# Rotary attention in front of two gated layers: how the first two head pairs are prepared, a second raw area, and a new order of the planned work

## The chip, the cores and the metric

One Trainium2 chip, of which the program uses one core. The metric is device time of one execution, in microseconds (us); of several executions the median is given. Lower is better.

## The reference

Inputs are q, k, v (4 batches, 8 heads, 576 positions, width 64), a dense gated layer and an eight-expert layer. Cut to what matters:

```python
q_rot, k_rot = (rotate(q), rotate(k))          # rotary: x*cos + swapped(x)*sin
scores = np.matmul(q_rot, k_rot.transpose(0, 1, 3, 2)) / sqrt(64)
attn = exp(scores - max) / (sum + 1e-9)
x = np.matmul(attn, v)                         # -> (2304, 512)
gate = 1 / (1 + exp(-(x @ w_gate)))            # 512 -> 1536
x = (gate * (x @ w_val)) @ w_out
e = argmax(x @ wg2 + bias[modality])           # one of 8 experts per token
out = prob[e] * (relu(x @ w1[e]) @ w2[e])
```

Everything is float32 outside. Inside, most factors are split into a high part in TensorE's fast 32-bit type and a remainder ("hi" and "lo"), and a product is the sum of hi·hi, lo·hi and hi·lo.

## The kernel before, in words

The program has three stages: attention for 16 head pairs (4 batches of 4 pairs), the gated layer, and routing with the experts. The change touches attention alone.

A **pair** is two heads side by side on 128 partitions, 64 for each. Its nine score **tiles** have 128 queries against 576 keys each: four for head 0, four for head 1, one for what is left of both. The steps of a pair, with the lines of the code as it was before:

- **Loads** (`plan_loads`, L344): raw q and k with a half-swapped copy of each, by SP's queue, into the area `sa` (`self.raw`), of which there is one. The load of pair p waits until the last reader of pair p−1 (`lo`) is through.
- **Preparation**: rotary products and their sum (L175, L177, L173), high part (L165, L397, L409), low part (L451, L399, L411). Scores want, in one operand, a head's high queries on its 64 partitions and the low ones on the other 64 (`q2`), against the high keys on both (`kh`); the low keys `kl` get a second product. From pair 2 on (`plan_prep`) both heads are split at once on 128 partitions, and six small DMAs (L461) put the parts where the scores want them. Pairs 0 and 1 (`plan_direct`) have no time for these DMAs: ACT and DVE write each part in its place, 64 partitions at a time.
- **Scores** (`scores`, L198): four or six matmuls of 288 columns into PSUM, two tiles in flight. For pair 0 the low keys are met by 64 partitions of queries, `(q[r], kl[r])`. DVE takes the scores out of PSUM with the row maximum (`evac_scores`, L208), ACT does the exponential with the row sum (L220).
- **Transposes** on TensorE (L251, L266), split by ACT (`pth`, L281) and DVE (`ptl`, L285); **values** (L298) in four groups per pair; ACT and DVE put them into `xy` (L306, L316, `value_add`).
- **Norm**: reciprocal of the row sums (L228), transposed and written out and read back along rows by DMA (L233, L504, L240), multiplied in (`normalise`, L245).
- **Fillers**: the conversion of the gated layer's first weights from 64-bit words (L650 to L685), and at the end the first two blocks of the gated layer (`early`, L725).

The **order** is set by a planner (`Plan`). Every step is entered with an engine, a cost, the steps that it needs and a priority; the planner goes through the program in modelled time and takes, on each engine, the ready step with the lowest number. The emitted order is fixed from then on: an engine runs its steps in that order and waits on semaphores for what is not there. The priorities come from a table of offsets (`PR`, `OFF`), and which engine does a movable step from other tables (`LO`, `VLO`, `ROPE`, `RM`, `HI`, `VHI`, `DIRECT`, `KLO`). DVE and POOL steps with two operands in SBUF are marked as shared: the planner lets only one of them run at a time.

Of the kernel before, what the change touches and what calls it, by code (L numbers as in the profile page):

```python
# [7 lines left out]
F32 = mybir.dt.float32  # L8
# [19 lines left out]
def f32(ap):  # L28
    return ap.bitcast(F32)
# [92 lines left out]
class Attention:  # L122
    def __init__(self, tc, pool, xpool, psum_s, psum_t, psum_v, qk, v, rope, ident, xt, rows, idle):
# [16 lines left out]
        self.raw = f32(sa[:, 0:4 * S]).rearrange("p (a s) -> p a s", a=4)  # L140
# [6 lines left out]
        self.vraw = t([128, 10, D], F32, "vraw")  # L147
        for i in range(2):
            nc.vector.memset(f32(self.q2[i][:, 0, S:640]), 0.0)
            nc.vector.memset(f32(self.q2[i][:, 1, 0:64]), 0.0)  # L150
            for x in range(2):
                nc.vector.memset(f32(self.w[i][64 - 64 * x:128 - 64 * x, S * x:S * x + S]), 0.0)
# [16 lines left out]
    def rope_op(self, eng, j, what, c=slice(0, S)):  # L169
        e = self.engine(eng)  # L170
        raw = self.raw
# [7 lines left out]
    def scores(self, T):  # L179

        nc = self.nc
# [4 lines left out]
        if t == 8:  # L188
            mm = [(q2[:, x, 512 * (1 - x):512 * (1 - x) + 128], kh[:, x]) for x in range(2)]
            mm.append((self.w[i][:, 512:640], kl))  # L190
        else:
            j, x = divmod(t, 2)
            r = slice(64 * x, 64 * x + 64)
            q = q2[:, x, 128 * (j + x):128 * (j + x) + 128]
            mm = [(q, kh[:, x]), (q[r], kl[r]) if p == 0 else (self.w[i][:, 640 * x + 128 * j:640 * x + 128 * j + 128], kl)]
# [141 lines left out]
    def plan_loads(self, p, load_rope=None, load_const=None):  # L337
        nc = self.nc
        b, hp = divmod(p, NP)
        at = TPP * (p - 2) + 1  # L340

        def ld(half, cols):
            h = slice(2 * half, 2 * half + 2)
            return lambda: nc.sync.dma_start(out=self.raw[:, h, cols], in_=self.qk[b, hp, :, h, cols])  # L344
# [11 lines left out]
    def plan_v(self, p):  # L356
# [5 lines left out]
        self.op(("vhi", p), eng, {"ACT": 0.62, "POOL": 0.76}[eng], lambda eng=eng: self.copy(eng, vv[:, :, 0], self.vraw),  # L362
                [("loadv", p)] + prev, pr)
        eng = self.VLO.get(p, "POOL")
        self.op(("vlo", p), eng, {"DVE": 0.74, "POOL": 1.58}[eng], lambda: self.engine(eng).tensor_tensor(
# [8 lines left out]
    def plan_direct(self, p, pr):  # L374

        nc = self.nc
        q2, kh, kl, w_, raw = self.q2[p], self.kh[p], self.kl[p], self.w[p], self.raw
        cost = lambda eng, w: {"DVE": 0.07 + w / 960, "POOL": 0.12 + w / 465, "ACT": 0.093 + w / 1200}[eng]
        r = [slice(0, 64), slice(64, 128)]
        every = {0: [], 1: []}  # L380
        need = {}
        for half in (1, 0):
            j = 2 * half
            for n, c in enumerate(self.cuts(p, half)):
                w = c.stop - c.start
                load = [("load", p, half, n)] + [("rope", i) for i in range(len(self.cuts(0, 1))) if c.stop > SH * i]
                for k, what in enumerate(("mul", "mul", "add")):
                    e = "POOL" if (p, half, n, k) in self.DIRECT else "DVE"
                    i = j + 1 - k if k < 2 else j
                    self.op(("rope", p, half, n, k), e, cost(e, w), lambda e=e, i=i, what=what, c=c: self.rope_op(e, i, what, c),  # L390
                            load if k < 2 else [("rope", p, half, n, 0), ("rope", p, half, n, 1)], pr + n)
                rot = [("rope", p, half, n, 2)]
                if half:
                    for x in range(2):
                        for y in range(2):
                            self.op(("khi", p, y, x, n), "ACT", cost("ACT", w),
                                    lambda x=x, y=y, c=c: nc.scalar.copy(out=kh[r[y], x, c], in_=raw[r[x], 2, c]), rot, pr + 1 + x + n)  # L397
                        e = "POOL" if (p, x, n) in self.KLO else "DVE"
                        self.op(("klo", p, x, n), e, cost(e, w), lambda e=e, x=x, c=c: self.engine(e).tensor_tensor(  # L399
                            out=kl[r[x], c], in0=raw[r[x], 2, c], in1=f32(kh[r[x], x, c]), op=ALU.subtract),  # L400
                            [("khi", p, x, x, n)], pr + 2 + x + n)
                        keys = [("khi", p, 0, x, n), ("khi", p, 1, x, n), ("klo", p, x, n)]
                        every[1] += keys
                        need.setdefault(("k", x), []).extend(keys)
                    continue
                for x in range(2):
                    i, o = c, slice(c.start + 64 * x, c.stop + 64 * x)
                    key = (p, x, c.start)
                    self.op(("qhi", *key), "ACT", cost("ACT", w), lambda x=x, o=o, i=i: nc.scalar.copy(  # L409
                        out=q2[r[x], x, o], in_=raw[r[x], 0, i]), rot, pr + 1.5 + x + n)  # L410
# [1277 lines left out]
```

## Time and profile before

| | us |
|---|---|
| median of 3 runs | 1044.75 (1043.98 to 1047.44) |
| the profiled execution | 1046.64 |
| its span, first to last instruction | 1044.8 |
| PE (TensorE) busy in the span | 990.2 (95%) |
| DVE (VectorE) busy | 673.5 (64%) |
| ACT (ScalarE) busy | 529.4 (51%) |
| POOL (GpSimd) busy | 360.1 (34%) |
| attention, up to the last value products | about 317 |

The shares are over the whole program. A stage is read from windows: there the busy time of each engine stands for one stretch of the span, with TensorE's granted clock (1.00 is the upper of its two levels, 2.4 GHz; 0.50 the lower, 1.2 GHz).

### The profile page before, as it was taken

What the parts mean: (1) busy time and instruction counts of PE and PEld (TensorE: products, weight loads), DVE (VectorE), ACT (ScalarE), POOL (GpSimd) and SP (SyncE); (2) the same over time, 40 slices, a digit from 0 to 9 for tenths busy, and PEclk for the clock granted to TensorE, in tenths of its full rate; (3) what the DMA queues carried; (4) which work ended last, traced back from release to release, by engine and by line L of the source; (5) the groups of instructions that cost most, each with busy time, mean ns of one, the idle gap of its engine ahead of it and who ended that gap; (6) DMA issues with size and microseconds to landing.
All of it is one profiled execution on the core that took longest, in us unless ns stands there. A gap on an engine that the chain in (4) does not pass through costs nothing.

```text
span 1044.8 us, 16293 instructions
## 1 busy us (share of the span) xinstructions
PE 990.2 (95%) x6035; PEld 912.2 (87%) x6035; DVE 673.5 (64%) x1208; ACT 529.4 (51%) x1042; POOL 360.1 (34%) x276
## 2 busy tenths in 40 slices
PE   4789999989999999999999999999987999999996
PEld 3779999888998999999999999999965899999995
DVE  7799999999997746545535535523376755555651
ACT  5889898988886522212212212223331645555542
POOL 2458768766412423223223323301151012111111
PEclk9899999999999999999999999999998899999998
DMA  5387776856311311101101101000046877666650
GB/s 193 105 224 211 191 197 175 227 165 181 106 65 63 101 41 42 62 21 61 41 21 61 42 20 61 21 1 2 1 137 186 307 228 232 221 222 223 222 170 24
DMA packets 66198, 127.23 MB, mean 122 GB/s; under 512 B 6511, under 2 KB 29695, under 8 KB 66112
## 3 DMA queue, kind: packets, MB, share of 16 engines
q1 hardware_dynamic: 52192, 108.55, 34.3%
q0 software_dynamic: 3040, 9.70, 2.7%
q10 hardware_dynamic: 10880, 7.87, 2.5%
q8 instruction: 49, 0.80, 0.3%
q14 instruction: 37, 0.30, 0.1%
HBM read 95.65 MB, written 9.77 MB: 101 GB/s over the span
## 4 chain that ended last, share of the span: by engine, by line
PE 53%; issue 18%; DVE 11%; DMA 7%; ACT 5%; POOL 3%; SPq 0%; ACTq 0%; POOLq 0%; DVEq 0%
PE gv L725 28%; PE yo L791 13%; DMA out<-e_y,r_si 5%; DVE e L208 3%; PE pv L298 3%; PE s L198 3%; DVE ptl L285 2%; ACT e L220 2%; PE pt L251 2%; ACT pth L281 1%; POOL e_xg L1456 1%; DMA sa<-in_qk 1%; DVE xy L316 1%; PE s L725 1%; PE r_pl L1225 1%
## 5 line engine op out<-in xcount | busy, mean ns | idle before, releaser
L734 POOL TENSOR_TENSOR gl<-sg,gh 128x384 fp32r<-128x384 f32 x60 | 63.5, 1059 | 259.0 <-ACT gh L733 259.0
L732 DVE TENSOR_TENSOR sg<-gv,sg 128x384 f32<-128x384 f32 x70 | 39.1, 558 | 142.0 <-PE gv L725 122.1
L220 ACT ACTIVATE e<-e,st 128x576 f32<-128x576 f32 x144 | 112.0, 781 | 17.9 <-DVE e L208 17.0
L1449 DVE TENSOR_TENSOR e_w<-wr,e_w 128x1024 fp32r<-128x1024 f32 x80 | 96.0, 1222 | 28.3 <-ACT e_w L1448 26.8
L208 DVE TENSOR_SCALAR_CACHE_REDUCE e<-s 128x576 f32<-128x576 f32 x144 | 105.2, 746 | 6.8 <-PE s L198 6.1
L731 ACT ACTIVATE sg<-gv 128x384 f32<-128x384 f32 x70 | 34.4, 491 | 144.8 <-PE gv L725 144.6
L251 PE MATMUL pt<-cst,e 128*128 128x128 f32 x576 | 83.1, 280 | 12.5 <-DVE ptl L285 7.1
L285 DVE TENSOR_TENSOR ptl<-pt,pth 128x512 fp32r<-128x512 f32 x144 | 93.3, 680 | 1.9 <-ACT pth L281 0.6
L1448 ACT CAST e_w<-wr 128x1024 fp32r<-128x1024 f32 x80 | 81.5, 1048 | 23.7 <-DMA x_rows<-xy 20.3
L198 PE MATMUL s<-sb 128*128 128x288 f32 x320 | 77.3, 333 | 16.3 <-DVE sb L411 12.1
L1504 PE MATMUL e_py<-e_w,e_hh 128*128 128x512 f32 x288 | 89.6, 392 | 0.0
L1519 POOL DMA_INDIRECT out<-e_y,r_si x19 | 19.6, 1030 | 188.3 <-ACT e_y L1518 177.9
L281 ACT CAST pth<-pt 128x512 fp32r<-128x512 f32 x144 | 79.1, 586 | 9.7 <-PE pt L251 9.0
L251 PEld LDWEIGHTS pt<-cst,e 128*128 128x128 f32 x576 | 69.1, 144 | 16.7 <-issue 5.5
L1486 PE MATMUL e_ph<-e_xh,e_w 128*128 128x256 f32 x576 | 82.4, 287 | 0.7 <-ACT e_xh L1469 0.7
L733 ACT CAST gh<-sg 128x384 fp32r<-128x384 f32 x60 | 30.8, 514 | 100.8 <-DVE sg L732 100.8
L298 PE MATMUL pv<-pth,vv 128*128 128x256 f32 (+1 forms) x256 | 74.2, 312 | 6.4 <-DVE xy L316 5.4
L725 PE MATMUL gv<-xe,wb 128*128 128x384 f32 x384 | 78.9, 338 | 0.0
L1486 PEld LDWEIGHTS e_ph<-e_xh,e_w 128*128 128x128 f32 x576 | 76.3, 195 | 1.7 <-ACT e_xh L1469 1.1
L725 PE MATMUL gv<-xh,wb 128*128 128x384 f32 x288 | 74.1, 338 | 0.0
L175 POOL TENSOR_TENSOR sa<-sa,rope 128x1152 f32<-128x1152 f32 x24 | 64.1, 2672 | 28.1 <-DMA sa<-in_qk 21.1
L198 PEld LDWEIGHTS s<-sb 128*128 128x128 f32 x320 | 51.2, 200 | 22.8 <-DVE sb L411 12.1
(247 smaller groups left out, 2471.5 us busy)
## 6 DMA issues: line engine op xcount, KB each, us to landing
wr<-in_w SPq DMA_DIRECT2D x74, 512.0 KB
sa<-in_qk SPq DMA_DIRECT2D x30, 576.0 KB
sb<-sa SPq DMA_DIRECT2D x56, 288.0 KB
wraw<-in_wg SPq DMA_DIRECT2D x12, 512.0 KB
wraw<-in_wv SPq DMA_DIRECT2D x12, 512.0 KB
wraw<-in_wo SPq DMA_DIRECT2D x12, 512.0 KB
vraw<-in_v SPq DMA_DIRECT2D x16, 320.0 KB
rr<-recip_rows SPq DMA_DIRECT2D x32, 144.0 KB
```

The lines of the kernel that those rows point to most:

```text
L198: nc.tensor.matmul(ps[:, u, 0:SH], a, m[:, SH * u:SH * u + SH], start=n == 0, stop=n == len(mm) - 1)
L208: self.nc.vector.tensor_scalar(out=e, in0=ps[:, :, 0:SH], scalar1=-0.125, scalar2=3.0e38, op0=ALU.mult, op1=ALU.min, accum_out=st[:, 0])
L220: nc.scalar.activation(out=e, in_=e, func=AF.Exp, bias=st[:, 0], scale=-1.0, accum_out=st[:, 1])
L251: nc.tensor.transpose(pt[:, c], e[:, 128 * c:128 * c + 128], self.ident)
L281: self.nc.scalar.copy(out=hi, in_=src)
L285: self.nc.vector.tensor_tensor(out=lo, in0=src, in1=f32(hi), op=ALU.subtract)
L298: nc.tensor.matmul(ps[:, 0:w], a, m, start=n == 0, stop=n == len(mm) - 1)
L725: self.nc.tensor.matmul(p[:, 0:U], a[:, wc], b[:, c], start=c == 0 and n == 0, stop=c == KC - 1 and n == 2)
L791: nc.tensor.matmul(ps, a, b, start=n == 0, stop=n == 3 * len(GROUPS[grp]) - 1)
L1449: nc.vector.tensor_tensor(out=lo, in0=raw, in1=f32(hi), op=ALU.subtract)
L1486: nc.tensor.matmul(ps[:, k], a[:, fs], b[:, c], start=n == 0, stop=n == 3 * KC - 1)
L1504: nc.tensor.matmul(ps, a[:, f, hs], b, start=n == 0, stop=n == 23)
```

## The change

- **Pair 0's queries** are kept as they lie: the high parts of both heads in one array of 128 partitions, the low parts in another, each written by one operation per piece. So that one head's keys do not meet the other head's queries, `kh` and the low keys (now `kl0`, in the area `w`) have zeros on the other 64 partitions. A tile is then six matmuls over 128 partitions (hi·hi, lo·hi, hi·lo), twelve for the last; high keys are copied once rather than twice. The zeros come from memsets, of which POOL now does some.
- **Unread products** (`warm`): 14 matmuls of 128 x 320 in plain float32 on zeros, ahead of the first score; nobody reads them.
- **Pair 1** goes the way of the later pairs (`plan_prep`), with products, sums and low parts on POOL and six placing DMAs. A tiny POOL addition (`first`) that reads pair 0's last results is put ahead of them, so that POOL starts on pair 1 only when pair 0 is prepared.
- **A second raw area** for odd pairs up to 11, in the part of `xy` that the last batch will fill: a load of pair p waits for pair p−2 there. Even pairs and the last four use `sa`.
- The priorities and the engine tables are **set anew**; the first two blocks of the gated layer get their planned ends behind the last values.

The diff, cut to its core:

```diff
-        self.raw = f32(sa[:, 0:4 * S]).rearrange("p (a s) -> p a s", a=4)
+        self.raws = [f32(sa[:, 0:4 * S]).rearrange("p (a s) -> p a s", a=4), xt[:, :, (B - 1) * S:B * S]]
...
+        nc.vector.memset(self.xv, 0.0)
+        o = [slice(64, 128), slice(0, 64)]
+        for x in range(2):
+            nc.vector.memset(f32(self.kh[0][o[x], x]), 0.0)
+            nc.vector.memset(f32(self.w[0][o[x], S * x:S * x + S]), 0.0)
...
+    def half_of(self, p):
+        return p % 2 if p < (B - 1) * NP else 0
...
+        if p == 0:
+            h, l, z = q2[:, 0], q2[:, 1, 64:640], self.kl[0]
+            if t < 8:
+                c = 128 * j + 64 * x
+                own = [(h[:, c:c + 128], l[:, c:c + 128], x)]
+            else:
+                own = [(h[:, 512:640], z[:, 128:256], 0), (z[:, 0:128], q2[:, 1, 0:128], 1)]
+            mm = [a for qh, ql, x in own for a in ((qh, kh[:, x]), (ql, kh[:, x]), (qh, self.kl0[x]))]
...
-                self.dma(("load", p, half, n), size, ld(half, cols), [("lo", p - 1, half)], at)
+                self.dma(("load", p, half, n), size, ld(half, cols), [("lo", q, half) for q in before], at)
...
-                        for y in range(2):
-                            self.op(("khi", p, y, x, n), "ACT", cost("ACT", w),
-                                    lambda x=x, y=y, c=c: nc.scalar.copy(out=kh[r[y], x, c], in_=raw[r[x], 2, c]), rot, pr + 1 + x + n)
+                        self.op(("khi", p, x, n), "ACT", cost("ACT", w),
+                                lambda x=x, c=c: nc.scalar.copy(out=kh[r[x], x, c], in_=raw[r[x], 2, c]), rot, pr + o_["kh"] + o_["x"] * x + o_["n"] * n)
...
+                self.op(("qhi", p, n), "ACT", cost("ACT", w), lambda hi=hi, c=c: nc.scalar.copy(out=hi, in_=raw[:, 0, c]),
+                        rot, pr + o_["qh"] + o_["n"] * n)
+                self.op(("qlo", p, n), "DVE", cost("DVE", w), lambda hi=hi, lo=lo, c=c: nc.vector.tensor_tensor(
+                    out=lo, in0=raw[:, 0, c], in1=f32(hi), op=ALU.subtract), [("qhi", p, n)], pr + o_["ql"] + o_["n"] * n)
...
+        self.op("first", "POOL", 0.1, self.first, every[0] + every[1], -500)
...
-    VLO = dict.fromkeys((2, 5, 6, 7, 12, 14, 15,), "DVE")
-    ROPE = dict.fromkeys(((2, 0), (3, 1), (4, 0), (11, 1),), "DVE")
+    VLO = dict.fromkeys((0, 4, 10, 12, 13,), "DVE")
+    ROPE = dict.fromkeys(((2, 0), (2, 1), (9, 1),), "DVE")
...
+    def warm(self, n=14):
+        ps = self.ps_t.tile([128, 512], F32, name="warm", tag="pt", bufs=PT_BUFS)
+        for _ in range(n):
+            self.nc.tensor.matmul(ps[:, 0:320], self.xv[:, 0:128], self.xv, start=True, stop=True)
...
-                if p + 1 < self.NDIRECT:
-                    self.plan_direct(1, 0.0)
-                else:
-                    self.plan_prep(p + 1)
+                self.plan_prep(p + 1)
```

Three places of the emitted order follow. In the names, `s` are score tiles in PSUM, `e` the scores out of it, `pt` and `ptl` transposed tiles and their low parts, `sb` holds `q2` and `kh`, `sa` the raw area, `w_99`/`w_100` the arrays `w`, `wr` borrowed weight space (there `kl` of pair 0 and `p5`).

TensorE (PE), the start of the program, as it was before the change:

```order
L198 MATMUL s<-sb 128x288 x2
L198 MATMUL s<-wr,sb 128x288 x2
L198 MATMUL s<-sb 128x288 x2
L198 MATMUL s<-wr,sb 128x288 x2
L198 MATMUL s<-sb 128x288 x2
```

The same engine and place now:

```order
L576 MATMUL warm<-xv 128x320 x14
L222 MATMUL s<-sb 128x288 x4
L222 MATMUL s<-w_99,sb 128x288 x2
L222 MATMUL s<-sb 128x288 x4
L222 MATMUL s<-w_99,sb 128x288 x2
```

Fourteen unread products now stand first, and a tile is four matmuls with `kh` and two with the low keys, where it was two and two.

DVE, between the middle score tiles of pair 0 and its transposed tiles, as it was:

```order
L208 TENSOR_SCALAR e,st<-s 128x576
L177 TENSOR_TENSOR sa<-sa,rope 128x576
L208 TENSOR_SCALAR e,st<-s 128x576 x2
L173 TENSOR_TENSOR sa<-sa 128x576
L177 TENSOR_TENSOR sa<-sa,rope 128x576
L285 TENSOR_TENSOR ptl<-pt,pth 128x4x128
L285 TENSOR_TENSOR wr<-pt_216,wr 128x256
L208 TENSOR_SCALAR e,st<-s 128x576
L399 TENSOR_TENSOR kl_98<-sa,sb 64x576
L208 TENSOR_SCALAR e,st<-s 128x576 x2
L411 TENSOR_TENSOR sb<-sa,sb 64x576 x2
L285 TENSOR_TENSOR ptl<-pt,pth 128x4x128 x3
```

DVE now, from pair 0's first score tile to its ninth:

```order
L390 TENSOR_TENSOR vv_95<-vraw,vv_95 128x10x64
L232 TENSOR_SCALAR e,st<-s 128x576 x5
L309 TENSOR_TENSOR ptl<-pt,pth 128x4x128
L232 TENSOR_SCALAR e,st<-s 128x576
L309 TENSOR_TENSOR ptl<-pt,pth 128x4x128
L309 TENSOR_TENSOR wr<-pt_246,wr 128x256
L232 TENSOR_SCALAR e,st<-s 128x576 x2
L309 TENSOR_TENSOR ptl<-pt,pth 128x4x128 x2
L232 TENSOR_SCALAR e,st<-s 128x576
L190 TENSOR_TENSOR sa<-sa,rope 128x1152
```

The six steps of pair 1 (L177, L173, L399, L411) are gone from between the evacuations; all nine tiles of pair 0 are taken out before a rotary product of pair 2 (L190).

POOL, its work from pair 0's low values on, as it was:

```order
L365 TENSOR_TENSOR vv_95<-vraw,vv_95 128x10x64
L177 TENSOR_TENSOR sa<-sa,rope 128x576 x2
L173 TENSOR_TENSOR sa<-sa 128x576
L399 TENSOR_TENSOR kl_98<-sa,sb 64x576
L365 TENSOR_TENSOR vv_96<-vraw,vv_96 128x10x64
```

POOL now, from its last step for pair 0 on:

```order
L188 TENSOR_TENSOR sa<-sa 128x320
L451 TENSOR_TENSOR order<-w_99,sb 128x2
L190 TENSOR_TENSOR xy<-xy,rope 128x2x576 x2
L188 TENSOR_TENSOR xy<-xy 128x576 x2
L473 TENSOR_TENSOR sa<-xy,sa 128x576
L473 TENSOR_TENSOR kl_98<-xy,sa 128x576
```

All of pair 1's products, sums and low parts now stand on POOL in one run, behind the tiny addition L451; their raw area is `xy`.

## Rows read from the trace of the kernel before

**Rows 1.** Windows: busy us (instructions) of each engine, granted clock, DMA share and rate

```profile
core 0: us, PE busy (x) PEld busy (x) DVE busy (x) ACT busy (x) POOL busy (x), PEclk, DMA share, GB/s
0.00:317.00 317.00, 281.80 (x2040) 264.62 (x2041) 291.36 (x653) 261.01 (x606) 189.17 (x124) 0.98 0.60 170
13.87:40.28 26.41, 20.38 (x73) 16.11 (x74) 20.22 (x37) 16.58 (x35) 10.25 (x7) 0.89 0.45 143
12.06:31.45 19.39, 17.96 (x58) 13.12 (x58) 14.78 (x31) 13.52 (x29) 7.97 (x5) 1.00 0.33 105
36.03:40.96 4.93, 4.90 (x22) 4.93 (x23) 3.39 (x6) 3.50 (x8) 1.84 (x2) 0.50 0.75 233
40.28:300.82 260.54, 243.53 (x1859) 232.31 (x1859) 248.96 (x565) 227.14 (x536) 173.96 (x110) 0.99 0.63 173
320.00:680.00 360.00, 359.51 (x1904) 337.86 (x1903) 194.56 (x290) 109.87 (x207) 104.37 (x91) 1.00 0.15 46
```

**Rows 2.** DVE group, 14 to 40.3 us (busy us, mean ns | idle before, releaser)

```profile
L208 DVE TENSOR_SCALAR_CACHE_REDUCE e<-s 128x576 f32<-128x576 f32 x10 | 7.5, 752 | 4.8 <-PE s L198 4.7
```

**Rows 3.** Timeline of PE: start us, length us, what; three places

```profile
30.10 1.10 PE L198 MATMUL s<-sb 128*128 128x288 f32 x4
39.56 0.68 PE L198 MATMUL s<-kl,w 128*128 128x288 f32 x2
298.41 0.77 PE L198 MATMUL s<-sb 128*128 128x288 f32 x4
```

**Rows 4.** DVE groups by shape, 0 to 310 us

```profile
L177 DVE TENSOR_TENSOR sa<-sa,rope 128x576 f32<-128x576 f32 x2 | 1.5, 752 | 0.0
L173 DVE TENSOR_TENSOR sa<-sa 128x576 f32<-128x576 f32 x5 | 3.8, 750 | 0.0
L399 DVE TENSOR_TENSOR kl<-sa,sb 64x576 fp32r<-64x576 f32 x1 | 0.7, 744 | 0.0
L411 DVE TENSOR_TENSOR sb<-sa,sb 64x576 fp32r<-64x576 f32 x2 | 2.9, 1438 | 0.1
L411 DVE TENSOR_TENSOR sb<-sa,sb 64x320 fp32r<-64x320 f32 x2 | 1.4, 707 | 0.1
L411 DVE TENSOR_TENSOR sb<-sa,sb 64x256 fp32r<-64x256 f32 x2 | 0.8, 419 | 0.1
L173 DVE TENSOR_TENSOR sa<-sa 128x320 f32<-128x320 f32 x1 | 0.5, 492 | 0.0
L175 DVE TENSOR_TENSOR sa<-sa,rope 128x1152 f32<-128x1152 f32 x4 | 6.3, 1566 | 0.1
L365 DVE TENSOR_TENSOR vv<-vraw,vv 128x640 fp32r<-128x640 f32 x7 | 6.2, 885 | 0.1
L451 DVE TENSOR_TENSOR sa<-sa 128x576 fp32r<-128x576 f32 x3 | 5.6, 1879 | 0.8 <-ACT sa L165 0.8
```

**Rows 5.** PE group of plain float32 products on constants, 320 to 1044 us

```profile
L1412 PE MATMUL e_ph<-cst 128*128 128x512 f32 x16 | 7.0, 592 | 0.0
```

**Rows 6.** POOL groups by shape, 0 to 310 us

```profile
L175 POOL TENSOR_TENSOR sa<-sa,rope 128x1152 f32<-128x1152 f32 x24 | 64.1, 2672 | 28.1 <-DMA sa<-in_qk 21.1 <-ACT e L220 5.3 <-DMA sb<-sa 1.7
L173 POOL TENSOR_TENSOR sa<-sa 128x576 f32<-128x576 f32 x25 | 36.9, 1477 | 2.8 <-DVE sa L177 2.0
L451 POOL TENSOR_TENSOR sa<-sa 128x576 fp32r<-128x576 f32 x11 | 16.3, 1483 | 13.7 <-ACT sa L165 13.3
```

**Rows 7.** Chain of waits, 200 to 240 us: a placing DMA in it

```profile
204.70 5.43 DMA sb<-sa
```

**Rows 8.** Timeline around 228 us, and the windows row behind it

```profile
226.17 2.67 POOL L175 TENSOR_TENSOR sa<-sa,rope 128x1152 f32<-128x1152 f32 x1 [5.32 <-ACT e L220]
226.64 2.81 DVE L451 TENSOR_TENSOR sa<-sa 128x576 fp32r<-128x576 f32 x1
...
230.79 1.25 PE L251 MATMUL pt<-cst,e 128*128 128x128 f32 x8 [2.29 <-DVE ptl L285]
...
231.79:235.50 3.71, 3.71 (x21) 3.52 (x20) 2.41 (x5) 1.74 (x4) 1.94 (x2) 0.55 1.02 283
```

More of the change, by code (lines that the diff above doesn't have):

```diff
@@ L167, in copy, with raw, rope_op @@
             self.nc.gpsimd.tensor_scalar(out=out, in0=in_, scalar1=1.0, scalar2=0.0, op0=ALU.mult, op1=ALU.add)
-    def rope_op(self, eng, j, what, c=slice(0, S)):
+    def half_of(self, p):
+        return p % 2 if p < (B - 1) * NP else 0
+    def raw(self, p):
+        return self.raws[self.half_of(p)]
+    def rope_op(self, eng, p, j, what, c=slice(0, S)):
         e = self.engine(eng)
-        raw = self.raw
+        raw = self.raw(p)
         if what == "add":
@@ L339, in plan_loads @@
         b, hp = divmod(p, NP)
-        at = TPP * (p - 2) + 1
+        at = TPP * p - self.PR["load"]
+        before = [q for q in range(p) if self.half_of(q) == self.half_of(p)][-1:]
         def ld(half, cols):
             h = slice(2 * half, 2 * half + 2)
-            return lambda: nc.sync.dma_start(out=self.raw[:, h, cols], in_=self.qk[b, hp, :, h, cols])
+            return lambda: nc.sync.dma_start(out=self.raw(p)[:, h, cols], in_=self.qk[b, hp, :, h, cols])
         for half in (1, 0) if p == 0 else (0, 1):
@@ L361, in plan_v @@
         eng = self.VHI.get(p, "ACT")
[L362 removed]
+        self.op(("vhi", p), eng, {"ACT": 0.62, "POOL": 0.70}[eng], lambda eng=eng: self.copy(eng, vv[:, :, 0], self.vraw),
                 [("loadv", p)] + prev, pr)
         eng = self.VLO.get(p, "POOL")
[L365 removed]
+        self.op(("vlo", p), eng, {"DVE": 0.74, "POOL": 1.53}[eng], lambda: self.engine(eng).tensor_tensor(
             out=vv[:, :, 1], in0=self.vraw, in1=f32(vv[:, :, 0]), op=ALU.subtract), [("vhi", p)], pr)
@@ L421, in plan_direct @@
                             need.setdefault((x, t), []).extend(keys)
-                    every[0] += keys
-                    last = slice(512 - 512 * x, S - 512 * x)
-                    if p == 0 and c.start <= last.start < c.stop:
-                        self.op(("qd", p, x), "ACT", 0.15, lambda x=x, last=last: nc.scalar.copy(
-                            out=w_[r[x], 512 + 64 * x:576 + 64 * x], in_=raw[r[x], 0, last]), rot, pr + 8)
-                        every[0].append(("qd", p, x))
+                every[0] += keys + [("qz", p, n)]
+        self.op("first", "POOL", 0.1, self.first, every[0] + every[1], -500)
         for half in range(2):
@@ L430, in plan_direct, with first @@
         self.ready[p] = [need[t % 2, t // 2] + need["k", t % 2] for t in range(8)] + [every[0] + every[1]]
+    def first(self):
+        self.nc.gpsimd.tensor_tensor(out=self.stat1, in0=f32(self.w[0][:, S - 1::S]), in1=f32(self.q2[0][:, 1, 319::320]), op=ALU.add)
     def plan_prep(self, p):
@@ L483, in plan_tile @@
         ready = self.ready[p][t]
-        self.op(("s", T), "PE", (0.81 if t == 8 else 0.54 if p else 0.92) * (1 if T > 4 else 2), lambda: self.scores(T), ready, T + o["s"], "s")
+        self.op(("s", T), "PE", 0.27 * (2 + (p == 0)) if t < 8 else 0.81 * (1 + (p == 0)), lambda: self.scores(T), ready, T + o["s"], "s")
         self.op(("tsa", T), "DVE", 0.665, lambda: self.evac_scores(T), [("s", T)], T + o["tsa"], "e")
@@ L773, in early @@
             gh, gl = (w[:, 0:U] for w in self.w[1][2 - u])
-            deps = [prev, ("post", u - 1, 3), "table"]
+            deps = [prev, ("post", u - 1, 3), "table"] + [("value", last, x, w) for x in range(2) for w in range(2)]
             for n, (eng, cost, _) in enumerate(self.gv_post(0, u, None, sg, gh, gl, "DVE")):
```

84 lines of the change are left out of this document (41 added, 43 removed).

## The prediction, made before the changed kernel ran

> **What bounds the kernel now.** I read the windows first [rows 1]. Behind 320 us TensorE is busy 359.5 of 360 us: what follows attention is bound by TensorE and does not change, so every microsecond by which attention ends earlier comes out at the end, and every one later too. In attention (0 to 317 us) it is DVE that is nearly full: 291.4 us busy, against 281.8 of TensorE and 261.0 of ACT. From 40 to 301 us DVE is idle for only 260.5 − 249.0 = 11.6 us, TensorE for 17, ACT for 33. So attention lasts as long as DVE's work and the gaps in it, and the question about each part of the change is what it does to these two.
>
> The gaps lie unevenly. From the first evacuation of scores (13.87 us) to the tenth, pair 1's first (40.28 us), DVE is idle 26.4 − 20.2 = 6.2 us [rows 1]; 4.7 us of that it waits for scores from TensorE [rows 2]. TensorE in turn is busy 18.0 of 19.4 us from 12 to 31 us, but slowly: four score matmuls of 288 columns take 1.10 us at 30.1 us and 0.77 us at 298.4 us [rows 3]. At 39.6 us two of them take 0.68 us [rows 3], in a stretch where the granted clock is 0.50, the lower level [rows 1]. The clock column reads 1.00 from 12 to 31 us, but the pace is that of the lower level, and I go by the pace.
>
> The Trainium skill weighs against this reading: "TensorE: Matmul & The Clock Gate" (Part 1, What's actually happening) says that TensorE starts throttled and that sustained matmul work releases it. By that rule, pair 0's own 19 us would have lifted the clock early, the unread products would buy nothing, and the sum below would lose its second term and come to −9.4 us. The trace does not agree: the pace at 30 us is still the slow one.
>
> **The change part by part, in DVE's time.**
>
> *Pair 1 leaves DVE.* Two rotary products of 576 columns (1.5 us), one sum (0.75), one low-key step (0.74) and two low-query steps (2.9) go to POOL: −5.9 us [rows 4].
>
> *Pair 0 in natural layout.* Four low-query pieces (1.4 + 0.8 = 2.2 us) become two with the same columns on twice the partitions. DVE's time follows columns here: a 128 x 320 sum takes 0.49 us, a 64 x 256 piece 0.42 [rows 4]. So the two cost between 0.84 and 1.4, I take 1.1. Two low-key pieces come over from POOL, at some 0.45 each (between the same rows), and a 128 x 320 sum goes to POOL (−0.5). Together −0.7 us.
>
> *The engine tables.* Rotary products on DVE go from four to three (−1.57) and their sums with them (−0.75); low values from seven to five (−1.8) [rows 4]. Low parts go from six to seven. Such a step takes 0.74 us where nothing holds it (the low-key step) and 1.88 us on average for three of them [rows 4]; I take 1.3. Together −2.8 us. The fifth of each, the normalisations on DVE, the evacuations and the splits keep their numbers.
>
> The first term is thus −5.9 − 0.7 − 2.8 = **−9.4 us**.
>
> *The unread products and the six-matmul tile.* TensorE has nothing to do until 12.06 us [rows 1]. Eight plain float32 products of 512 columns took 7.0 us at the upper level [rows 5], so 14 of 320 take 7.0 × 4480/4096 = 7.7 us there, and twice that, 15.3, at the lower. They can start once DVE has zeroed the operand, a little after 1 us. In the one stretch that shows a return, the clock came back after 4.9 us of work (36.03 to 40.96 us) [rows 1]; with that I get about 5 us at the lower level, 5 at the upper, and an end near 11.3 us, ahead of the first score. If so they cost nothing; their cover is TensorE's wait for pair 0's preparation, and if it is shorter than they are, the excess delays every score. A tile of six matmuls takes at the upper level under 0.77 × 6/4 = 1.2 us (the row holds the time in which the last result comes out, which the next tile covers), near DVE's 0.75 for taking one out [rows 2, 3]; at the lower level up to 1.10 × 6/4 = 1.65. Of the 4.7 us that DVE waited for scores, then, between 0 and 4.7 return. I take 4.0, since nothing else in that stretch made it wait for long: second term **−4.0 us**.
>
> *Pair 1 on POOL.* In POOL's queue stand two double products, two sums and two low parts: 2 × 2.67 + 2 × 1.48 + 2 × 1.48 = 11.3 us [rows 6]. They begin behind the tiny addition, when pair 0's low parts are there, near 14 us, and end near 25. Six placing DMAs follow on SP, one issue behind the other, and one such transfer stood 5.4 us in the chain of waits [rows 7]: pair 1's scores can start between 29 and 34 us. DVE has pair 0's nine evacuations, nine splits, two products and two sums of pair 2 ahead of pair 1's first tile in the new order; without gaps that is 19 us of work, to about 34. So the DMAs hide, just. What is late next if they don't is pair 1's first tile, and TensorE idles. I cost it at zero, with 0 to 4 us kept for the range. POOL is off the path otherwise (189 of 317 us busy [rows 1]).
>
> *The second raw area* takes away POOL's waits for loads (21.1 us [rows 6]). No engine that is full waits for POOL there, so I cost it at nothing: it lets preparation run ahead.
>
> *ACT* gets five more high parts of values and loses some ten copies of pairs 0 and 1; with 33 us of slack [rows 1] this is nothing.
>
> *The new order* between 40 and 301 us has no price in any row. Its bounds are DVE's idle time there: it could return all of 11.6 us, or add as much. I take zero, the middle, as both orders come from the same planner.
>
> **The sum:** −9.4 − 4.0 = −13.4 us. The profiled execution took 1046.64 us, so it becomes 1033.2. The median of the runs shown is 1044.75, 1.9 us lower, and against it I predict **1031.3 us**. A check inside: DVE's tenth evacuation near 35 us, not 40.3. A measurement of this kernel can tell some 0.3%, about 3 us, from no change.
>
> **Rivals.**
>
> *POOL holds DVE (slower).* At 226 us a rotary product on POOL took 2.67 us, and a low part that DVE began 0.5 us later took 2.81 us instead of 0.74; TensorE then idled 2.3 us and came back at the lower level, granted clock 0.55 from 231.8 to 235.5 us [rows 4, 8]. One such hold costs DVE 2.1 us. The change gives POOL pair 1 as well, and leaves DVE some twenty two-operand steps to be caught. From 13.4/2.1, between six and seven holds more than now, nothing is left of the gain; eight more give 1031.3 + 16.8 = 1048. For it: every step keeps a place that only a modelled time sets. Against it: DVE has fewer such steps than before. The Trainium skill states the mechanism as a rule ("SBUF — State Buffer", Who interferes with whom): a DVE instruction with two SBUF inputs and a POOL instruction that reads SBUF exclude each other for the whole instruction. The trace agrees, by the 2.81 us.
>
> *The clock does not rise.* The products stay at the lower level, end near 16.6 us, delay the first score by 4.5 us, and pair 0 keeps the slow pace. Then the second term is lost and 4.5 us added: −9.4 + 4.5 = −4.9, 1040. For it: the slow pace held for 19 us of work in the present trace. Against it: these products are dense and of full height, as the work from 36 us on was.
>
> *The slow pace had another cause than the clock*, as by the rule above: the scores of pair 0 came slowly because of their 64-partition products, and with six full ones per tile TensorE is no faster. The second term is lost, the first stands: 1044.75 − 9.4 = 1035.3. Against it: full products at 30.1 us were as slow [rows 3].
>
> *The gain is taken back.* The new order makes DVE wait in 40 to 301 us for what it gained at the start, through ACT or through placing DMAs: idle time there doubles, +11.6, and 1043 comes out, no change.
>
> *The new order is also tighter.* Half to all of the 11.6 us go as well: 1020 to 1026.
>
> **How the numbers follow.** Forecast (1026 to 1038) 0.60; slow pace of another cause (1035.3) 0.06; tighter order 0.12; clock that does not rise 0.09; gain taken back 0.07; POOL holds DVE 0.06. Faster by over 0.3% are the first four: 0.87; same 0.07; slower 0.06. The range of 8 in 10 reaches from 1023 (part of the tighter order) to 1040 (the clock rival's own value); it leaves out the last two cases and the far ends of the others.
>
> **What would show it.** Right: score matmuls of pair 0 at the upper pace from 12 us on; DVE idle under 3 us before the tenth evacuation, and that near 35 us; DVE's busy time up to the last value products near 282 us instead of 291; from 320 us on the same times, shifted by 13. Wrong: low parts and normalisations on DVE of 2 to 3 us each with TensorE idle behind them; a long wait of TensorE for pair 1's placing DMAs; unread products that still run when the first queries are ready; or an attention that ends as before, with the idle time moved.

## The result, and the profile after

The changed kernel takes 1033.46 us (median of 4 executions, 1032.35 to 1034.64) beside 1044.88 before: ratio 0.9887, interval 0.9865 to 0.9909. Predicted were 1031.3 us and 1023 to 1040. The profiled execution took 1034.64 us, against 1033.2 of the sum. Against its own median the change brings 1044.88 − 1033.46 = 11.4 us, where 13.4 was forecast. Single executions of one kernel lie several us apart (before: 1042 to 1054 on one chip), so below medians are compared for the end, and profiles stretch by stretch.

The windows of the changed kernel: from the start to the first product of the next gated layer, from the first to the tenth evacuation, from there to the last, and from there to that first product.

```profile
core 0: us, PE busy (x) PEld busy (x) DVE busy (x) ACT busy (x) POOL busy (x), PEclk, DMA share, GB/s
0.00:307.56 307.56, 289.12 (x2108) 270.24 (x2108) 281.58 (x646) 260.14 (x605) 196.93 (x131) 0.99 0.65 179
14.42:35.67 21.25, 18.02 (x123) 16.58 (x123) 17.86 (x38) 15.82 (x36) 15.00 (x10) 0.92 0.61 177
35.67:281.15 245.48, 234.63 (x1787) 223.31 (x1788) 232.79 (x544) 221.47 (x522) 175.77 (x108) 0.99 0.70 188
281.15:307.56 26.41, 24.69 (x161) 22.38 (x159) 20.19 (x45) 17.97 (x40) 2.57 (x2) 1.00 0.18 53
```

The same first stretch of the kernel before, which reached its first product of the gated layer at 321.01 us, and its last stretch, from the last evacuation to that product:

```profile
0.00:321.01 321.01, 285.32 (x2058) 267.43 (x2058) 293.82 (x659) 263.78 (x610) 189.17 (x124) 0.98 0.59 168
300.82:321.01 20.19, 19.61 (x125) 17.75 (x123) 15.05 (x34) 13.20 (x28) 2.72 (x2) 1.00 0.21 68
```

The next layer begins 321.01 − 307.56 = 13.45 us earlier; the sum said 13.4. In this execution it is made up otherwise than the sum: DVE works 293.82 − 281.58 = 12.2 us less (−9.4 predicted) and idles 27.2 − 26.0 = 1.2 us less (−4.0 predicted). A second profile of the same kernel, below, splits its 14.0 us as 9.1 and 4.9, so one profile does not settle the split. By stretches, 5.2 us went from the first to the tenth evacuation and 15.1 from there to the last (260.5, [rows 1], to 245.5; 16.2 of DVE's work), while the last stretch grew by 6.2 us (20.19 to 26.41), where TensorE now works 24.69 us instead of 19.61, and the first evacuation came 0.55 later. What follows took 725.1 us instead of 723.8. The granted clock falls there in both kernels, at different places (after the change between 772 and 804 us and again from 1024 us on; before it between 768 and 816 us and from 1036 on); that these falls make the difference was not shown.

The DVE groups that answer to [rows 4], and one more of before (the normalisations) behind them:

```profile
L390 DVE TENSOR_TENSOR vv<-vraw,vv 128x640 fp32r<-128x640 f32 x5 | 5.3, 1054 | 0.0
L269 DVE TENSOR_TENSOR xy<-xy,rr 128x576 f32<-128x576 f32 x5 | 5.1, 1023 | 0.0
L473 DVE TENSOR_TENSOR sa<-sa 128x576 fp32r<-128x576 f32 x2 | 4.7, 2336 | 0.0
L190 DVE TENSOR_TENSOR sa<-sa,rope 128x1152 f32<-128x1152 f32 x2 | 2.8, 1418 | 0.0
L190 DVE TENSOR_TENSOR xy<-xy,rope 128x1152 f32<-128x1152 f32 x1 | 1.4, 1361 | 0.0
L433 DVE TENSOR_TENSOR sb<-sa,sb 128x256 fp32r<-128x256 f32 x1 | 1.1, 1082 | 0.0
L192 DVE TENSOR_TENSOR sa<-sa,rope 128x320 f32<-128x320 f32 x2 | 0.9, 482 | 0.0
```

```profile
L245 DVE TENSOR_TENSOR xy<-xy,rr 128x576 f32<-128x576 f32 x5 | 6.3, 1263 | 0.0
```

Five normalisations cost 1.2 us less though nothing about them changed; the rotary products are shorter too, the low values longer (1054 ns each, 885 in [rows 4]). POOL seems to hold some of DVE's steps less often in the new order and others more, and the clock does not fall near 232 us as in [rows 8]. Where it does hold DVE, the prices are as before: two low parts of 2336 ns, and a low query of 1082 ns that would take some 0.42.

TensorE at the start, with its score products at line 222:

```profile
1.26 9.69 PE L576 MATMUL warm<-xv 128*128 128x320 f32 x28 [1.26 <-DVE xv L148]
11.55 0.53 PE L222 MATMUL s<-sb 128*128 128x288 f32 x2 [0.60 <-ACT sb L431]
13.86 0.42 PE L222 MATMUL s<-w,sb 128*128 128x288 f32 x2
15.23 1.26 PE L222 MATMUL s<-sb 128*128 128x288 f32 x4 [0.95 <-DVE e L232]
33.57 0.52 PE L222 MATMUL s<-sb 128*128 128x288 f32 x2 [0.87 <-DMA sb<-sa]
35.70 0.55 PE L322 MATMUL pv<-pth,vv 128*128 128x320 f32 x1 [0.62 <-DVE xy L340]
```

and the windows behind two of its gaps:

```profile
16.00:18.00 2.00, 2.00 (x11) 2.00 (x9) 0.77 (x2) 1.03 (x4) 2.00 (x2) 0.50 0.97 386
36.00:38.00 2.00, 2.00 (x9) 2.00 (x9) 1.12 (x4) 1.53 (x4) 2.00 (x3) 0.50 0.92 335
```

The unread products end at 10.95 us (11.3 predicted) and the first scores run at the upper pace. Behind the wait of 0.95 us the clock falls to the lower level, and once more behind the waits near 33 and 35 us, the first of them for pair 1's placing DMAs. The prediction did not have these falls.

### The profile page after: what moved, and what is told of

It reads as the page before. It is cut to its first block, busy times and chain, and to the rows that moved or that the text cites. A ratio compares the mean times of both kernels' runs of the same rounds, so it can differ in the third digit from the quotient of the medians.

```text
span 1032.7 us, 16362 instructions
## 1 busy us (share of the span) xinstructions
PE 994.0 (96%) x6085; PEld 914.7 (89%) x6085; DVE 661.2 (64%) x1195; ACT 525.6 (51%) x1037; POOL 368.2 (36%) x283
## 4 chain that ended last, share of the span: by engine, by line
PE 53%; issue 14%; DVE 6%; DMA 6%; ACT 5%; POOL 1%; SPq 1%; ACTq 0%; POOLq 0%; DVEq 0%
PE gv L752 28%; PE yo L818 13%; DMA out<-e_y,r_si 5%; PE pv L322 2%; ACT e L244 2%; PE e_ph L1513 2%; ACT pth L305 2%; PE s L222 1%; PE pt L275 1%; DVE e L232 1%; PE e_py L1531 1%; DVE ptl L309 1%; PE r_pl L1252 1%; POOL e_xg L1483 1%; PE r_pt L1216 1%
## 5 line engine op out<-in xcount | busy, mean ns | idle before, releaser
L244 ACT ACTIVATE e<-e,st 128x576 f32<-128x576 f32 x144 | 112.1, 782 | 12.7 <-DVE e L232 12.0
L275 PE MATMUL pt<-cst,e 128*128 128x128 f32 x576 | 80.2, 275 | 5.0 <-DVE ptl L309 3.7
L275 PEld LDWEIGHTS pt<-cst,e 128*128 128x128 f32 x576 | 66.9, 141 | 8.9 <-DVE ptl L309 4.7
L322 PE MATMUL pv<-ptl,vv 128*128 128x256 f32 (+1 forms) x256 | 70.5, 298 | 0.0
L752 PEld LDWEIGHTS gv<-xe,wb 128*128 128x128 f32 x384 | 67.1, 188 | 1.2
```

The costliest lines, as they stand in the source:

```text
L244: nc.scalar.activation(out=e, in_=e, func=AF.Exp, bias=st[:, 0], scale=-1.0, accum_out=st[:, 1])
L275: nc.tensor.transpose(pt[:, c], e[:, 128 * c:128 * c + 128], self.ident)
L322: nc.tensor.matmul(ps[:, 0:w], a, m, start=n == 0, stop=n == len(mm) - 1)
L752: self.nc.tensor.matmul(p[:, 0:U], a[:, wc], b[:, c], start=c == 0 and n == 0, stop=c == KC - 1 and n == 2)
```

## The experiments

Two theories stood at the start of the experiments. The forecast's: attention lasts as long as DVE's work and gaps; the unread products and pair 1 on POOL bring the gain, the second area and the new numbers are worth nothing by themselves. The rival: the parts hang together, and the gain comes from the new order and the area that allows it.

**One unread product.** `for _ in range(n)` in `warm` becomes `for _ in range(1)`; the order keeps its place for fourteen.

> The changed kernel with one unread product in place of fourteen, the order of all else unchanged. If the unread products are what keeps the clock up for pair 0: scores start at the lower level, a tile of six products takes 1.44 us (three pairs of 0.48) and not 0.8, the tenth evacuation moves from 35.7 to 39 us or later, and the end moves by +3.5 to +5 us, to 1037 to 1038.5. If full-height scores lift the clock by themselves within 5 us: three or four tiles are slow, +1 to +2 us, 1034.5 to 1035.5. If TensorE's pace does not matter there because DVE is the bound: within 1 us of 1033.5.

Measured: 1032.45 us, ratio 0.9869 (0.9838 to 0.9900): no loss. The timeline of TensorE:

```profile
12.97 0.85 PE L222 MATMUL s<-sb 128*128 128x288 f32 x2 [0.32 <-DVE sb L433]
14.10 1.17 PE L222 MATMUL s<-sb 128*128 128x288 f32 x4
17.09 1.12 PE L222 MATMUL s<-sb 128*128 128x288 f32 x4
18.05 0.43 PE L222 MATMUL s<-w,sb 128*128 128x288 f32 x2
18.68 0.77 PE L222 MATMUL s<-sb 128*128 128x288 f32 x4
```

Pairs of products (a pair here: the two matmuls of 288 columns that share their queries) follow each other after 0.48 us up to 18.05 us and after 0.27 behind it: the pace rose after 5 us of scores without a gap, the one unread product lying 9 us behind. First to tenth evacuation takes 20.83 us. The forecast's own reading (clock stays low, +3.5 to +5) falls; the middle one holds for the pace, not for the end.

**More unread products**, in the gap near 14.5 us:

```
+        for _ in range(3 if T == 1 else 0):
+            nc.tensor.matmul(ps[:, 0, SH:512], self.xv[:, 0:128], self.xv[:, 0:512 - SH], start=True, stop=True)
         self.s[T] = ps
```

> The changed kernel with three more unread products (224 columns) behind the second tile's scores, in the gap of 0.95 us after which the clock fell at 15.4 us. If that gap is what lost the clock: granted clock 1.00 from 10 to 32 us, no wait of DVE for scores over 0.3 us between 16 and 20 us (now 1.16, 0.67 and 0.69), tenth evacuation 1 to 2 us earlier, end 1031.5 to 1032.5. If the clock falls for another reason, or DVE has other work that waits anyway: tenth evacuation and end within 0.5 us of the changed kernel's.

Measured: 1032.34 us, ratio 0.9873 (0.9839 to 0.9906). No fall of the clock up to 750 us, first to tenth evacuation 20.02 us, tenth at 34.88: the early mechanism as expected, the end within the noise. Near 36 us the clock did not fall here, though nothing was put there.

**Pair 1 on DVE**: its six preparation steps are issued on DVE at the places in the order that they had on POOL, `self.rope_op("DVE" if p == 1 else eng, ...)` and likewise for the low parts.

> The changed kernel with pair 1's rotary products, sums and low parts (six instructions, 2 x 1.4 + 4 x 0.74 = 5.8 us) on DVE, at the places in the order that they had on POOL. If DVE's work and gaps set attention's length, and the gap near 37 us, where pair 1 comes late, goes: +3.4 to +5.8 us, 1037 to 1039. If POOL's late preparation of pair 1 costs as much as it saves DVE: within 1.5 us of 1033.5.

Measured: 1038.07 us, ratio 0.9908 (0.9874 to 0.9941), 5.6 and 5.7 us above the two versions before, on the same chip. The page's line of busy times, of this version and, second, of the changed kernel:

```profile
PE 995.3 (96%) x6085; PEld 915.0 (88%) x6085; DVE 667.0 (64%) x1201; ACT 526.1 (51%) x1037; POOL 358.0 (35%) x277
PE 994.0 (96%) x6085; PEld 914.7 (89%) x6085; DVE 661.2 (64%) x1195; ACT 525.6 (51%) x1037; POOL 368.2 (36%) x283
```

DVE works 667.0 us instead of 661.2: +5.8. Beside the two versions on the same chip the end moves by about as much, and so does the first product of the gated layer (309.95 us; 304.59 and 304.85 in those two). Beside the changed kernel's own two profiles (307.56 and 306.98 us), from other chips, that product moves by 2.4 and 3.0 us only. That work put on DVE comes out at the end is shown; that it does so one for one is not.

**The early gate products as before**: `gv=-51.05, post=869.62`, and the dependence on the last value products taken out of `early`.

> The changed kernel with the old numbers for the early gate products and without their new dependence on the last value products, so that all 48 stand ahead of the last value products, as before the change. If the 3.4 us by which the last value products gained more than the first gate products of the next layer (16.9 against 13.45) was lost at this place: first gate products near 304 us, end near 1030. If TensorE is full there anyway and only its idle time counts (0.6 us from 281 to 301.5, 1.1 us from there to 307.6): 0 to -1.5 us, 1032 to 1033.5.

Measured: 1034.30 us, ratio 0.9879 (0.9847 to 0.9911). From the last evacuation to the first product of the gated layer:

```profile
279.81:308.62 28.81, 24.42 (x161) 22.58 (x159) 21.16 (x45) 18.17 (x40) 2.58 (x2) 1.00 0.16 48
```

28.81 us instead of 26.41, with the same work for TensorE. The stretch also began 1.3 us earlier here, so the first product of the gated layer is 1.1 us later (308.62 us, 307.56 in the changed kernel). Nothing was lost by the new place of the gate products. Both expectations missed.

**The unread products alone on the kernel before** (`warm` and its operation added, `xv` zeroed; all else stays in its order).

> The kernel before with the fourteen unread products alone put ahead of its first scores (and their operand zeroed), nothing else changed. If the products were what lifted TensorE's pace for pair 0: first score tiles at the upper pace and to stay there, first to tenth evacuation 22 to 23 us (26.4 before, 21.3 with the whole change), end 3.5 to 4.5 us earlier than before. If half-height score products do not keep the pace up: a few tiles at the upper pace, then the lower one, first to tenth evacuation 25 us or more, end within 1.5 us of before.

Measured: 1046.55 us beside 1047.78, ratio 0.9981 (0.9963 to 1.0000). First to tenth evacuation, and TensorE at three places:

```profile
14.62:40.36 25.74, 19.02 (x74) 15.34 (x74) 19.07 (x38) 16.01 (x33) 9.21 (x7) 0.63 0.47 147
```

```profile
14.97 0.53 PE L199 MATMUL s<-wr,sb 64*128 64x288 f32 x2
15.44 0.53 PE L199 MATMUL s<-sb 128*128 128x288 f32 x2
...
25.37 0.84 PE L199 MATMUL s<-wr,sb 64*128 64x288 f32 x2
26.15 0.85 PE L199 MATMUL s<-sb 128*128 128x288 f32 x2
```

The old score tiles mix products of 128 and of 64 rows, and a pair of them takes 0.46 us at the upper pace and 0.78 at the lower. So an old tile of two pairs takes 0.92 us at the upper pace and 1.55 at the lower; the new one of three full pairs takes 0.8 and 1.44. The same pair takes 0.78 us in the kernel before:

```profile
14.39 0.85 PE L198 MATMUL s<-wr,sb 64*128 64x288 f32 x2
15.17 0.85 PE L198 MATMUL s<-sb 128*128 128x288 f32 x2
```

The pace fell back behind a wait of 0.82 us, near 18 us, and stayed low behind one of 1.68. But the products' operand is zeroed later here than in the changed kernel: they start at 4.35 us instead of 1.26, and the first score comes at 13.46 us instead of 12.06. The tenth evacuation stands where it was (40.36 us, 40.28 before). What they would bring to this kernel if they started at 1.26 us is not shown.

**Full-height products on the kernel before**: `(q[r], kl[r]) if p == 0` becomes `(q, kh[:, x]) if p == 0`. Pair 0's scores then leave out the low keys.

> The kernel before with pair 0's products of 64 rows (queries by low keys) replaced by a second product of 128 rows by the high keys, so that pair 0's scores leave out the low keys; no unread products, order unchanged. If the half-height products kept TensorE at the slow pace: the pace rises within 5 to 6 us of the first score, near 18 us, as it did with one unread product; first to tenth evacuation 22 to 24 us and the end 2.5 to 4 us earlier than before. If the slow pace came from something else (short gaps, pair 1's work on DVE): pace slow to 31 us as before, first to tenth evacuation 26 us or more, end within 1 us of before.

Measured: first to tenth evacuation 21.68 us instead of 26.41,

```profile
14.11:35.79 21.68, 14.95 (x73) 13.30 (x71) 19.91 (x38) 16.20 (x34) 9.30 (x7) 0.92 0.41 128
```

```profile
17.18 2.26 PE L198 MATMUL s<-sb 128*128 128x288 f32 x8 [0.91 <-DVE e L208]
24.26 1.93 PE L198 MATMUL s<-sb 128*128 128x288 f32 x8
```

nearly as much as the whole change brings there, with neither unread products nor pair 1 on POOL. DVE's idle time in the stretch fell from 6.2 to 1.8 us. The pace rose near 26 us rather than 18 (waits of 0.9 and 2.1 us lay between), so most of pair 0 ran at the lower pace here too: two tiles of four products in 2.26 us, where two mixed ones took 3.1. What was won there came from the height of the products. The profiled execution took 1041.13 us, but the median of twelve is 1046.82, ratio 0.9978 (0.9956 to 1.0000): four lie near 1042, eight at 1044.7 or more. Why most executions give this gain back is open; only one of the four was profiled.

**One raw area** in the changed kernel: `half_of` returns 0.

> The changed kernel with one raw area for all pairs, as before the change; the order comes from the same numbers, planned anew. If the second area is worth nothing, as in the prediction: POOL waits for loads some 21 us again (13 now) and the end stays within 1.5 us of the changed kernel's. If preparation that runs ahead is what keeps DVE's and TensorE's queues filled: DVE's idle time from the tenth to the last evacuation grows by 3 us or more, and so does the end.

Measured: 1068.13 us, ratio 1.0206 (1.0175 to 1.0238), slower than before by 20 us: the second reading, and far beyond its 3 us. From the tenth to the last evacuation, and POOL's rotary products up to 300 us:

```profile
37.74:325.50 287.76, 252.43 (x1821) 233.69 (x1822) 253.30 (x564) 230.04 (x536) 180.07 (x110) 0.96 0.59 165
```

```profile
L190 POOL TENSOR_TENSOR sa<-sa,rope 128x1152 f32<-128x1152 f32 x27 | 74.0, 2742 | 43.0 <-DMA sa<-in_qk 39.9 <-DVE ptl L309 2.5 <-DMA wraw<-in_wg 0.6
```

POOL waits 39.9 us for loads, DVE idles 34.5 us in this stretch instead of 12.7. The new numbers, which were set for two areas, depend on the second.

**Gaps filled**: the products of the second experiment (two, not three), and four of 128 columns on the identity ahead of the tenth and behind the eleventh score tile.

```
+        for _ in range(4 if T == 9 else 0):
+            nc.tensor.matmul(ps[:, 0, SH:SH + 128], self.ident, self.ident, start=True, stop=True)
         for n, (a, m) in enumerate(mm):
...
+        for _ in range(4 if T == 10 else 0):
+            nc.tensor.matmul(ps[:, 0, SH:SH + 128], self.ident, self.ident, start=True, stop=True)
         self.s[T] = ps
```

> The changed kernel with further unread products in the gaps of TensorE's queue near 14.5 us (two of 224 columns), 33 us and 35 us (four of 128 columns each). If the gaps cost the clock: granted clock 1.00 from 10 to 750 us, first to tenth evacuation 19.5 to 20 us, tenth to thirteenth 3.4 us (5.1 now), end 2 to 3 us earlier, 1030.5 to 1031.5. If the clock falls there for another reason, or falls in some executions only: profile as the changed kernel's or better by one fall, median within 1 us.

Measured: 1029.02 us (1028.23 to 1031.61), ratio 0.9820 (0.9797 to 0.9843), the best of all medians. The stretches are now 19.70 and 244.02 us:

```profile
14.48:34.18 19.70, 18.18 (x140) 16.78 (x139) 18.05 (x39) 15.65 (x36) 14.96 (x10) 1.00 0.63 181
34.18:278.20 244.02, 233.30 (x1792) 221.99 (x1791) 233.71 (x542) 221.57 (x522) 176.27 (x108) 1.00 0.70 190
```

The granted clock shows no fall up to 760 us, and the tenth to thirteenth evacuation take 3.74 us, 3.4 expected, 5.07 in the changed kernel.

**The changed kernel again**, and **filled gaps with one product ahead** (`range(1)` in `warm`), on one chip:

> The changed kernel itself, beside the runs that follow on the same chip. Ratio to before 0.987 to 0.990 as in the first measurement. Its profile shows whether the two falls of the clock (near 15 and 36 us) come in every execution: the variants that left its first 16 us alone showed one or both or none of them, so a profile with another pattern is expected as often as not.

> The version with filled gaps, with one of the fourteen products ahead of the first scores left. If the fourteen are what a start at the upper pace needs: first to tenth evacuation 1 us longer than with them (19.7 with filled gaps), end 1 us later, 1030. If filled gaps are enough: within 0.5 us of the version with filled gaps (1029.0), and the fourteen are worth nothing there.

Measured: 1032.46 us, ratio 0.9844 (0.9812 to 0.9876), below the 0.987 to 0.990 expected, and 1035.79, ratio 0.9883 (0.9856 to 0.9909). The changed kernel's second profile has no early fall of the clock at all:

```profile
0.00:306.98 306.98, 286.63 (x2107) 267.18 (x2108) 284.71 (x646) 260.34 (x605) 197.34 (x131) 1.00 0.65 179
14.24:33.93 19.69, 16.44 (x123) 15.04 (x123) 18.01 (x38) 15.64 (x36) 14.93 (x10) 1.00 0.65 186
33.93:280.55 246.62, 233.87 (x1787) 221.85 (x1788) 235.76 (x542) 221.82 (x522) 176.24 (x108) 1.00 0.70 188
```

The falls belong to the execution, not to the kernel, and 1.56 us won in the first stretch here shrank to 0.58 at the first product of the gated layer (306.98 us). Up to there DVE works 293.82 − 284.71 = 9.1 us less than before the change and idles 4.9 us less. With one product ahead and the gaps filled, the first stretch is

```profile
14.70:35.56 20.86, 19.65 (x146) 18.29 (x145) 17.97 (x38) 15.82 (x36) 15.01 (x10) 1.00 0.62 183
```

20.86 us, 1.2 longer than with fourteen (19.70), as the first reading had it. With open gaps it is the same: 20.83 us with one, 19.69 with fourteen where the clock did not fall. At the end, filled gaps with one product come out 6.8 us above those with fourteen, though with open gaps one and fourteen were even; so much the first stretch does not explain. Filled gaps with fourteen and with one were measured on different chips, and the profile with one also has a fall of the clock near 245 us. Whether filled gaps beat the changed kernel is open (the intervals, 0.9797 to 0.9843 and 0.9812 to 0.9876, overlap).

**The start alone**: layout, products, pair 1's products and sums on POOL, with the old tables, numbers and early gate products, once with one raw area, once with two (the last line of the diff only in the first). The old table of low parts has no entry for pair 1, so its two low parts run on DVE in both, not on POOL as in the changed kernel.

```
-    PR = dict(..., load=-692.82, ahead=972.28, k=-886.15, split=-1993.33, v=-512.72)
+    PR = dict(..., load=17, ahead=-166.37, k=-502.20, split=-1447.19, v=-640.88)
...
-        return p % 2 if p < (B - 1) * NP else 0
+        return 0
```

> The start of the change alone: natural layout, unread products and pair 1 on POOL, with one raw area and the old engine tables, order numbers and early gate products. By the prediction's sum (engine tables -2.8, second area 0, order numbers 0) it lacks 2.8 us of the gain: ratio to before near 0.990, some 1036. If the stretch from the tenth to the last evacuation, which lost 15 us with the change, owes that to the second area and the new numbers: that stretch takes 258 us or more again (260.5 before, 245.5 with the change), and the ratio is 0.994 to 1.000.

> The same with the second raw area. If the area is worth nothing by itself: within 1.5 us of the version with one area. If it is what lets preparation run ahead and takes DVE's steps out from under POOL's: tenth to last evacuation 5 us or more shorter than with one area, POOL's waits for loads under 15 us.

Measured: 1056.25 us with one area, ratio 1.0089 (1.0060 to 1.0119), slower than either reading allowed, and 1049.18 with two, 1.0014 (0.9989 to 1.0038). With one area:

```profile
13.50:40.62 27.12, 20.35 (x145) 18.03 (x143) 19.65 (x43) 17.07 (x40) 15.37 (x9) 0.99 0.56 166
40.62:306.47 265.85, 240.48 (x1789) 225.69 (x1790) 249.13 (x557) 223.88 (x523) 172.76 (x109) 0.98 0.66 176
```

```profile
28.69 0.75 DVE L473 TENSOR_TENSOR sa<-sa 128x576 fp32r<-128x576 f32 x1
39.11 0.50 PE L222 MATMUL s<-sb 128*128 128x288 f32 x2 [3.93 <-DMA sb<-sa]
```

```profile
L390 DVE TENSOR_TENSOR vv<-vraw,vv 128x640 fp32r<-128x640 f32 x7 | 10.1, 1447 | 0.0
```

With two:

```profile
13.75:40.22 26.47, 20.08 (x146) 18.08 (x145) 22.85 (x44) 16.75 (x40) 19.07 (x11) 1.00 0.59 171
40.22:290.87 250.65, 234.76 (x1770) 221.24 (x1771) 237.78 (x549) 221.19 (x519) 168.44 (x107) 0.99 0.69 181
```

```profile
30.06 0.74 DVE L473 TENSOR_TENSOR sa<-xy,sa 128x576 fp32r<-128x576 f32 x1
38.13 0.53 PE L222 MATMUL s<-sb 128*128 128x288 f32 x2 [1.13 <-DMA sb<-sa]
```

Pair 0's nine evacuations run fast in both (13.5 to 23.3 and 13.75 to 23.6 us), and then pair 1 comes late: first to tenth evacuation is as long as before the change. Its last low part ends on DVE at 29.44 and 30.80 us (26.75 on POOL in the changed kernel), and between its placing DMAs on SP stand loads of the next pairs; which of the two costs more was not tried. With one area DVE's work over the whole kernel is 674.1 us, no less than the 673.5 of before, although all of pair 1 but its low parts has left it: seven low values take 10.1 us (6.2 before, [rows 4]). The four long ones, 1.5 to 2.6 us each, all run into a two-operand step of POOL. That is what the prediction's POOL rival describes. The second area takes 15.2 us out of the middle stretch and 6.0 out of DVE's work (668.1), and 7 us out of the median. It does not do so by POOL's waits: its rotary products wait 46.9 us for loads with two areas (under 15 expected) and 52.4 with one. The two-area version lies in two groups (four executions at 1042 to 1046, eight at 1048.5 to 1052); the profile is of the first.

## Why the prediction was right, and where it was not

*Attention lasts as long as DVE's work and gaps*: right in the main. Six steps put back on DVE, 5.8 us of work, moved the first product of the gated layer by 2.4 to 5.4 us, depending on the run that they are set beside. DVE's busy time up to the last value products is 278.2 and 281.3 us in the two profiles (near 282 forecast).

*Pair 1 leaves DVE, −5.9*: right, 5.8 by that run, and POOL ended pair 1 at 26.75 us (near 25 predicted). *Hidden, just*: its scores waited 0.87 us for the placing DMAs at 33.57 us, inside the 29 to 34 us and the 0 to 4 us given. What was missed is how much this hangs on the tables and the order: with the old ones pair 1's first scores came 4.6 and 5.5 us later.

*Natural layout −0.7 and engine tables −2.8*: the counts of steps were right, their lengths only on the whole. The steps that the prediction priced, pair 1 with them, fell by 9.2 us in the first profile (−9.4 predicted) and by 5.9 in the second, added up from the DVE groups: the low values came to 5.3 and 7.0 us (4.4 predicted), the low parts to 10.2 and 11.6 (10.7 predicted). Steps that it had left at nothing fell by another 2.6 us in both (normalisations −1.2, conversions of weights −0.8, pair 0's rotary products −0.6). In pair 0 alone the low queries came to 1.6 us (1.1 predicted), because POOL's sum held one for 1.08.

*The second term, −4.0*: before the tenth evacuation DVE idled 3.4 us instead of 6.2 in the profiled execution (−2.8), 1.7 in the other one (−4.5). The size was fair, the cause was not: "the pace is that of the lower level" was read rightly, but the step that followed, that without the unread products the pace stays there, failed. With full-height scores it rose after 5 us, and thirteen of the fourteen unread products are worth 1.1 us of the first stretch (20.83 to 19.69 us) and nothing that the end shows. What helped is the layout: full products instead of mixed ones, which cost 0.46 us a pair even at the upper pace. In the kernel before, full products alone took DVE's idle time there to 1.8 us in the profiled execution, though the median fell by 0.2% only. The row that the prediction read, 1.10 us at 30.1 us, is of the ninth tile, whose first four products are full; the eight tiles of 128- and 64-row products in turn, at 1.55 us each, it did not look at. Six full products are the cheaper tile at either level, 0.8 and 1.44 us, within the bounds that it gave (1.2 and 1.65). The Trainium skill's rule ("TensorE: Matmul & The Clock Gate", What's actually happening), that sustained matmul work releases the throttle, was set aside in the prediction because pair 0's 19 us had not done it; with full-height products the runs agree with it (0.48 us a pair, then 0.27 from 18.05 us on).

*The second raw area, 0*: wrong. Without it the new numbers cost some 35 us, and with the old numbers it is worth 7 us in the median. "No engine that is full waits for POOL there" looked at waits alone: where POOL's steps fall also sets how long DVE's take (with the old numbers seven low values took 10.1 us with one area, 8.3 with two).

*The new order, 0*: not shown to hold, and not taken apart. With the old numbers and tables and both areas, the kernel is 16.7 us slower in the median than the changed one on the same chip, and no faster than before the change. Pair 1 comes late there (26.5 us from the first to the tenth evacuation instead of 21.3), and DVE works 668.1 us instead of 661.2. About 4.5 of these 6.9 us are steps that the old tables put on DVE (a rotary product and its sum, two low values, a low part, at unheld length); what the order numbers bring without the tables was not run.

*From 320 us on the same times, shifted by 13*: right at the start (13.45), 12.1 at the end.

So that the sum hit −13.45 with −13.4 was in part luck. In the first profile two errors offset each other, 2.8 us too little of DVE's work and 2.8 us too much of its idle time; in the second the two terms are near (−9.1 and −4.9), but of the first only 5.9 us come from the steps that were priced. A change whose parts were priced one by one came out right as a whole, while the prices of the second area and of the unread products did not hold by themselves.

## What to carry to other kernels

Where an engine's work sets the time, price a moved step by its unheld length; six steps of 5.8 us moved what follows by 2.4 to 5.7 us here. Don't price an order or a buffer at nothing because nobody waits for it in the old trace: test the parts together with the numbers that place them, since a start that runs ahead is worth nothing if the next pair comes late. And before blaming the clock for slow products, compare their form: products of 64 rows in turn with 128 were slower at either level than full ones. One profile of each kernel was not enough to say how DVE's time splits into work and waiting.

## What the runs showed that was not expected

- The clock column reads 1.00 from 12 to 18 us in the version with one unread product, while a pair of products takes 0.48 us, the length that in the changed kernel goes with 0.50 (16 to 18 us). At the start of an execution the pace is the safer sign.
- The same kernel, twice profiled, had falls of the clock at 15 and 36 us once and none the other time, with gaps of 0.9 to 1.0 us in TensorE's queue in both.
- Half-height and full products in turn take 0.46 us a pair at the upper pace and 0.78 at the lower, full ones 0.27 and 0.48.
- Fourteen unread products cost nothing in the changed kernel, where they end at 10.95 us, ahead of the first score. They shorten the first stretch by 1.1 us, which the end does not show.
